# Second weight of an expert's last 32 of 288 tokens: 32-row fp32r products replaced by plain fp32 partial products at four column positions

## The chip, the cores and the metric

The kernel runs on one core of one Trainium2 chip. The metric is device microseconds from start to end of one execution. The engines are TensorE (PE; its weight loads are shown apart as PEld, its sequencer's own instructions as PEldq), VectorE (DVE), ScalarE (ACT), GpSimd (POOL) and SyncE (SP), which issues the large DMA transfers.

## The reference

Three stages: windowed attention with 32 global tokens per batch entry, a channel mix, and a routed layer of eight experts with one expert per token. The change concerns the last one:

```python
    logits = np.einsum('bsd,de->bse', x, w_gate)
    local_gate = 1.0 / (1.0 + np.exp(-np.einsum('bsd,de->bse', x, w_local).squeeze(-1)))
    ...
            if s == 0 or local_gate[b, s] < 0.5:
                e = fresh_e
            else:
                e = prev_e if prev_e >= 0 else fresh_e
            ...
            h = np.maximum(x[b, s] @ w1[e], 0.0)
            out[b, s] = p[e] * (h @ w2[e])
```

There are 4 x 544 = 2176 tokens of 512 numbers; `w1[e]` is 512x1024, `w2[e]` is 1024x512. How many tokens an expert has is known only on the chip, after routing.

## The kernel before

Attention, channel mix and routing fill the first 500 us or so, laid out by a scheduler at build time. Behind them the experts run one after the other, in an order written out by hand (class `Experts`).

**Three products for one.** A product of this stage keeps nearly fp32 accuracy by splitting both factors into a high part (rounded to fp32r) and a low part (the rest): `mm3` issues high x high, high x low and low x high into one PSUM tile, on lines 21, 23 and 24. Every such group of matmuls in the trace carries these three lines. `slot0h`/`slot0l` to `slot3h`/`slot3l` are the two parts of a weight matrix; an expert uses two slots (`w1` and `w2`) while the next expert's weights are converted into the other two.

**One expert.** `expert` first takes tokens by 32s: chains of `If` on the count `c` choose one arm. With 257 to 288 tokens that is `joined(288)`; other arms are `joined(320)`, `joined(352)`, `joined(256)`, `single`, `none` and `big`. Each of the five middle experts has the whole chain in its code. In this run expert 2 has 267 tokens and is the only one in `joined(288)`. The arm has these steps:

- `begin`: copies of indices, and the gather of the next expert's rows (L940, GpSimd).
- `wide`: the first weight, eight steps `f`; in each 12 matmuls of up to 288 columns into `ph`, then ScalarE writes the high part of relu (`hh`, L969) and VectorE the low part (`hl`, L970).
- `out_(0,e,2,slice(256,N))`: the second weight for the tokens from 256 on. `product` makes 24 matmuls whose stationary factor is 128 x 32 (32 tokens) and whose moving factor is the weight, 512 columns; `place` scales the rows by the gate's probability on VectorE (L1007, PSUM bank `po0` to `osb`) and scatters them from GpSimd (L1010).
- `second`: the same for tokens 128 to 255 into bank `po1`, 24 matmuls of 128 rows.

Then comes the jump out of the arm, L1066, taken by each engine's own sequencer. Behind the whole chain of `If`s, for all arms, stand the eviction of bank `po1` and the third product: tokens 0 to 127 into bank `po0`, with the next expert's last transposes (`third`, L955 and L956) inside. TensorE then goes on to the next expert's first weight.

**Weights meanwhile.** `W` is a list of weight parts of 128x1024 (`whole`). One takes a staged part (`st` or `sw`), converts the high half on ScalarE (L853), subtracts on VectorE or, for some, on GpSimd (L856), and issues the next load of 512 KB on SyncE (L843) into the staging tile just freed. Up to three parts are called inside `wide`, two inside `second` at `f` = 0 and 2, three in the third product.

The two lines that call the arm's second weight:

```python
            if N>256: s.out_(0,e,2,slice(256,N))
            second(W[:2])
```

## Time and profile before

| | |
|---|---|
| median of three runs (lowest, highest) | 728.1 us (727.04, 732.19) |
| the profiled execution | 728.47 us, span of its instructions 726.7 us |
| TensorE matmul busy | 671.5 us, 92% of the span |
| TensorE weight load busy | 573.6 us, 79% |
| VectorE, ScalarE, GpSimd busy | 459.0 (63%), 368.5 (51%), 316.5 (44%) us |
| mean granted TensorE clock | 0.966 |
| DMA | 76.36 MB, mean 105 GB/s |

The profile is one execution. Busy times are sums over overlapping records, so shares are averages over stages with different limits; in the expert stage TensorE has hardly any gap. A matmul's record is longer than the pace at which matmuls follow one another (0.39 us beside 0.23), since they overlap; costs are taken from the distance of starts. [...]

### The profile page before, as it was taken

What the parts mean: (1) busy time and instruction counts of PE and PEld (TensorE: products, weight loads), DVE (VectorE), ACT (ScalarE), POOL (GpSimd) and SP (SyncE); (2) the same over time, 40 slices, a digit from 0 to 9 for tenths busy, and PEclk for the clock granted to TensorE, in tenths of its full rate; (3) what the DMA queues carried; (4) which work ended last, traced back from release to release, by engine and by line L of the source; (5) the groups of instructions that cost most, each with busy time, mean ns of one, the idle gap of its engine ahead of it and who ended that gap; (6) DMA issues with size and microseconds to landing.
All of it is one profiled execution on the core that took longest, in us unless ns stands there. A gap on an engine that the chain in (4) does not pass through costs nothing. (4 is left out here: it accounts for less than half of the span.)

```text
span 726.7 us, 14139 instructions
## 1 busy us (share of the span) xinstructions
PE 671.5 (92%) x4890; PEld 573.6 (79%) x4890; DVE 459.0 (63%) x1370; ACT 368.5 (51%) x938; POOL 316.5 (44%) x446
## 2 busy tenths in 40 slices
PE   3876879899999999989998999999899999999996
PEld 2654668688897897878987898877688899989785
DVE  5587668867878588694478654786744426234461
ACT  4677666765465764556652423426553316125251
POOL 6486764833635437255224413204734414322441
PEclk9789879999999999999999999999999999999999
DMA  5766144153112332111051000318864705406530
GB/s 115 210 167 200 32 112 133 54 108 61 43 29 60 66 64 51 32 24 40 16 173 60 1 30 15 117 44 271 308 249 147 248 18 189 157 21 229 183 103 22
DMA packets 111743, 76.36 MB, mean 105 GB/s; under 512 B 88910, under 2 KB 93006, under 8 KB 111634
## 3 DMA queue, kind: packets, MB, share of 16 engines
q1 hardware_dynamic: 108178, 64.28, 30.9%
q0 software_dynamic: 3456, 10.75, 4.1%
q8 instruction: 53, 0.87, 0.5%
q14 instruction: 56, 0.46, 0.2%
HBM read 66.08 MB, written 9.44 MB: 104 GB/s over the span
## 5 line engine op out<-in xcount | busy, mean ns | idle before, releaser
L259 POOL TENSOR_SCALAR pl<-pl,mx 128x192 f32<-128x192 f32 (+1 forms) x128 | 68.4, 552 | 84.6 <-DVE mx L256 71.6
L21 PE MATMUL psk<-xs,slot0h 128*128 128x256 f32 x256 | 75.1, 296 | 0.0
L23 PE MATMUL psk<-xs,slot0h 128*128 128x256 f32 x256 | 74.2, 290 | 0.0
L24 PE MATMUL psk<-xs,slot0l 128*128 128x256 f32 x256 | 73.5, 288 | 0.0
L253 ACT ACTIVATE pl<-pl,mx 128x224 f32<-128x224 f32 (+1 forms) x128 | 58.6, 459 | 26.7 <-DVE mx L249 25.9
L511 POOL TENSOR_SCALAR xm<-xT,mut 128x256 f32<-128x256 f32 (+4 forms) x96 | 44.2, 479 | 52.4 <-DVE kl L531 16.0
L969 ACT ACTIVATE hh<-ph 128x256 fp32r<-128x256 f32 (+2 forms) x56 | 22.4, 400 | 73.5 <-PE ph L24 47.0
L518 POOL TENSOR_TENSOR xs<-xm,xs 128x512 fp32r<-128x512 f32 (+1 forms) x36 | 45.8, 1287 | 28.2 <-ACT xs L516 18.1
L21 PE MATMUL psv<-slot1h,kh 128*128 128x512 f32 x136 | 54.4, 403 | 0.2 <-DVE kr L527 0.2
L23 PE MATMUL psv<-slot1l,kh 128*128 128x512 f32 x136 | 54.1, 398 | 0.5 <-POOL slot1l L485 0.5
L24 PE MATMUL psv<-slot1h,kl 128*128 128x512 f32 x136 | 53.6, 395 | 0.0
L266 PE MATMUL ptp<-ident,pl 128*128 128x128 f32 x256 | 43.9, 296 | 7.7 <-POOL pl L259 3.7
L970 DVE SCALAR_TENSOR_TENSOR hl<-ph,hh 128x256 fp32r<-128x256 f32 (+2 forms) x56 | 24.7, 442 | 40.9 <-ACT hh L969 40.7
L21 PEld LDWEIGHTS psk<-xs,slot0h 128*128 128x128 f32 x256 | 49.8, 197 | 0.8 <-ACT xs L516 0.6
L23 PEld LDWEIGHTS psk<-xs,slot0h 128*128 128x128 f32 x256 | 49.5, 193 | 0.8 <-issue 0.5
L24 PEld LDWEIGHTS psk<-xs,slot0l 128*128 128x128 f32 x256 | 49.5, 193 | 0.0
L514 DVE SCALAR_TENSOR_TENSOR xm<-xT,mut,xm 128x256 f32<-128x256 f32 (+4 forms) x96 | 44.1, 497 | 4.8 <-POOL xm L511 4.7
L114 ACT ACTIVATE ph<-ptp 128x512 f32<-128x512 f32 x64 | 37.2, 587 | 15.3 <-PE ptp L266 15.1
L266 PEld LDWEIGHTS ptp<-ident,pl 128*128 128x128 f32 x256 | 31.1, 150 | 15.2 <-POOL pl L259 5.4
L940 POOL DMA_INDIRECT xs<-y,idx x23 | 26.0, 1130 | 34.3 <-DVE cint L766 18.4
L21 PE MATMUL ph<-xh,slot2h 128*128 128x256 f32 (+1 forms) x128 | 37.1, 290 | 2.3 <-issue 1.6
L24 PE MATMUL ph<-xh,slot2l 128*128 128x256 f32 (+1 forms) x128 | 36.5, 285 | 0.0
(613 smaller groups left out, 2167.8 us busy)
## 6 DMA issues: line engine op xcount, KB each, us to landing
st<-in_moe_w_dram SPq DMA_DIRECT2D x42, 512.0 KB, 4.8
sw<-in_moe_w_dram SPq DMA_DIRECT2D x22, 512.0 KB, 4.8
y<-r SPq DMA_DIRECT2D x17, 256.0 KB, 2.1
earlyh<-in_moe_w_k_dram SPq DMA_DIRECT2D x8, 512.0 KB, 4.0
raw<-in_moe_w_v_dram SPq DMA_DIRECT2D x8, 512.0 KB, 4.3
ve<-in_v_l_dram SPq DMA_DIRECT2D x32, 96.0 KB, 2.1
bq<-in_q_l_dram SPq DMA_DIRECT2D x16, 128.0 KB, 2.8
bk<-in_k_l_dram SPq DMA_DIRECT2D x16, 128.0 KB, 2.9
```

Of the source, the lines that this page charges most:

```text
L21: i=nc.tensor.matmul(out,wh,xh,start=first,stop=False)
L23: nc.tensor.matmul(out,wh,xl,start=False,stop=False)
L24: return nc.tensor.matmul(out,wl,xh,start=False,stop=last)
L114: s.made=nc.scalar.activation(out[0],x,AF.Copy).ins.name
L253: nc.scalar.activation(p[:,h,ks],p[:,h,ks],AF.Exp,bias=mx[:,h:h+1],scale=-1.0,accum_out=mx[:,4+h:5+h])
L259: nc.gpsimd.tensor_scalar(out=p[:,h,ks],in0=p[:,h,ks],scalar1=mx[:,6+h:7+h],scalar2=0.0,op0=ALU.mult,op1=ALU.add)
L266: nc.tensor.transpose(pt[:,c,h],p[:,h,c*96:c*96+P],s.ident)
L511: nc.gpsimd.tensor_scalar(out=x[:,u,o:o+k],in0=s.xT[b][:,c,q:q+k],scalar1=m[:,1,c:c+1],scalar2=0.0,op0=ALU.mult,op1=ALU.add)
L514: nc.vector.scalar_tensor_tensor(out=x[:,u,o:o+k],in0=s.xT[b][:,c,1+q:1+q+k],scalar=m[:,0,c:c+1],in1=x[:,u,o:o+k],op0=ALU.mult,op1=ALU.add)
L518: nc.gpsimd.tensor_sub(xl[:,cs,:n],x[:,:,:n],xh[:,cs,:n].bitcast(F32))
L940: s.nc.gpsimd.indirect_dma_start(out=s.xs[i][:,j,:],out_offset=None,in_=s.y,in_offset=IndirectOffsetOnAxis(ap=s.idx[:,ch:ch+1],axis=0))
L970: nc.vector.scalar_tensor_tensor(out=hl[:,f],in0=ph,scalar=0.0,in1=hh[:,f].bitcast(F32),op0=ALU.max,op1=ALU.subtract)
```

## The change

In `joined(288)` the separate product of the last 32 tokens goes away, with its eviction and scatter ahead of `second`. In its place `left` makes two closures, `parts` and `whole`. VectorE first adds `hh` and `hl` of those tokens to one plain fp32 tile `h` (128x8x32), and sums the identity over four blocks of 32 columns to a selection `sel` (128x32, a 1 where row and column agree modulo 32). `parts`, called inside the second product after `f` = 3, issues 16 plain fp32 products: chunks `f+0` to `f+3` of the hidden dimension go to four column positions of the array (rows 0, 32, 64, 96 of the PSUM tile `phl`), once with the weight's high and once with its low half, for `f` = 0 and 4. ScalarE copies the 128x512 partial sums to `osl`. `whole`, called after `f` = 6, multiplies `sel` with `osl` in one plain fp32 product (`phs`), which adds the four partial sums; VectorE scales by the probability and GpSimd scatters. The two weight parts stay at `f` = 0 and 2 of the second product.

```diff
--- before.py
+++ after.py
@@ -1013,6 +1013,28 @@
         return s.pcol[:,ch:ch+1],s.idx[:,ch:ch+1]
     def out_(s,b,e,c,js=slice(0,P),within={}):
         s.product(b,e,js,within); s.place(b,*s.cols(e,c),n=js.stop-js.start)
+    def left(s,e):
+
+        nc=s.nc; n=32; w2=s.views(e,1); hh,hl=[t[:,:,2*P:2*P+n].bitcast(F32) for t in s.h]; J=P//n
+        w=s.work.tile([P,512],F32,tag="osb",name="hw",bufs=2); h=w[:,:8*n].rearrange("p (f t) -> p f t",f=8); sel=w[:,8*n:9*n]
+        nc.vector.tensor_tensor(out=h,in0=hh,in1=hl,op=ALU.add)
+        nc.vector.tensor_reduce(out=sel,in_=s.ident.rearrange("p (j t) -> p t j",j=J),axis=X,op=ALU.add)
+        o=[]
+        def parts():
+            ps=s.ps.tile([P,512],F32,tag="ph",name="phl",bufs=4)
+            for f in range(0,8,J):
+                for q in range(2):
+                    for j in range(J):
+                        nc.tensor.matmul(ps[j*n:(j+1)*n],h[:,f+j],w2[q][:,f+j].bitcast(F32),start=f==0 and q==0,stop=f==8-J and q==1)
+            o.append(s.work.tile([P,512],F32,tag="osb",name="osl",bufs=2))
+            nc.scalar.activation(o[0],ps,AF.Copy)
+        def whole():
+            ps=s.ps.tile([P,512],F32,tag="ph",name="phs",bufs=4)[:n]
+            nc.tensor.matmul(ps,sel,o[0],start=True,stop=True)
+            pc,idx=s.cols(e,2); t=s.work.tile([P,512],F32,tag="osb",name="osb",bufs=2)[:n]
+            nc.vector.tensor_scalar(out=t,in0=ps,scalar1=pc[:n],scalar2=None,op0=ALU.mult)
+            s.scatter(t,idx[:n])
+        return parts,whole
     def one(s,i,e,b,W,X,o=None):
 
         W=list(W); n=3 if e==1 else 5; last=s.tall(i,e,[W.pop(0) for _ in range(min(n,len(W)))],lead=1 if e==1 else None)
@@ -1053,6 +1075,10 @@
         def joined(N):
             begin()
             s.wide(i,e,N,W[:3],X)
+            if N==WJ[0]:
+                parts,whole=s.left(e)
+                s.product(1,e,slice(P,2*P),{0:W[:1],2:W[:1],3:[parts],6:[whole]})
+                return
             if N>256: s.out_(0,e,2,slice(256,N))
             second(W[:2])
         def single():
```

How it moves instructions is seen in three places. TensorE, from the end of the first weight into the second weight, before (`po_6734` is bank `po0`, `po_6735` bank `po1`):

```order
L23 MATMUL po_6734<-slot0l,hh 32x512 [waits Pool_49]
L24 MATMUL po_6734<-slot0h,hl 32x512 [waits DVE_49]
L21 MATMUL po_6734<-slot0h,hh 32x512 [waits Activation_49]
L23 MATMUL po_6734<-slot0l,hh 32x512
L24 MATMUL po_6734<-slot0h,hl 32x512 [waits DVE_49]
L21 MATMUL po_6735<-slot0h,hh 128x512
L23 MATMUL po_6735<-slot0l,hh 128x512
```

The same engine in the changed kernel, from step `f` = 3 of the second product on (`hw` is the VectorE tile that holds `h` and `sel`):

```order
L21 MATMUL po_6735<-slot0h,hh 128x512 [waits Activation_49]
L23 MATMUL po_6735<-slot0l,hh 128x512
L24 MATMUL po_6735<-slot0h,hl 128x512
L1028 MATMUL phl<-slot0h,hw 32x512 [waits DVE_49]
L1028 MATMUL phl<-slot0h,hw 32x512 x3
L1028 MATMUL phl<-slot0l,hw 32x512 x4
L1028 MATMUL phl<-slot0h,hw 32x512 x4
L1028 MATMUL phl<-slot0l,hw 32x512 x2
L1028 MATMUL phl<-slot0l,hw 32x512 [waits Pool_49]
L1028 MATMUL phl<-slot0l,hw 32x512
L21 MATMUL po_6735<-slot0h,hh 128x512 [waits Activation_49]
L23 MATMUL po_6735<-slot0l,hh 128x512
```

The second product now follows the first weight directly, and the products of the 32 tokens stand in its middle, in place of 24 matmuls ahead of it.

TensorE at the end of the arm, before:

```order
L24 MATMUL po_6735<-slot0h,hl 128x512
L21 MATMUL po_6735<-slot0h,hh 128x512
L23 MATMUL po_6735<-slot0l,hh 128x512
L24 MATMUL po_6735<-slot0h,hl 128x512
L1066 UNCONDITIONAL_BRANCH
```

and in the changed kernel, where the jump has become line 1092:

```order
L21 MATMUL po_6735<-slot0h,hh 128x512 [waits Activation_49]
L23 MATMUL po_6735<-slot0l,hh 128x512
L24 MATMUL po_6735<-slot0h,hl 128x512
L1033 MATMUL phs<-osl,hw 32x512 [waits DVE_49,Activation_49]
L21 MATMUL po_6735<-slot0h,hh 128x512
L23 MATMUL po_6735<-slot0l,hh 128x512
L24 MATMUL po_6735<-slot0h,hl 128x512
L1092 UNCONDITIONAL_BRANCH
```

A product that waits for ScalarE's copy now stands four instructions ahead of the jump.

GpSimd in this arm, before (the two L940 rows are the gather of the next expert's rows):

```order
L940 DMA xs_5166<-y,idx 128x512 [waits DMASW1_49,PE_49]
L940 DMA xs_5166<-y,idx 128x512 [waits DMASW2_49,PE_49]
L1010 DMA out_dram<-osb,idx 2176x512 [waits DMASW3_49,DVE_49]
L856 TENSOR_TENSOR slot1l<-sw_6725,slot1h 128x1024 [waits DMAHW5_49,DMAHW0_49,Activation_49]
L1066 ISA [waits DMASW1_49]
L1066 UNCONDITIONAL_BRANCH
```

and in the changed kernel:

```order
L940 DMA xs_5166<-y,idx 128x512 [waits DMASW1_49,PE_49]
L940 DMA xs_5166<-y,idx 128x512 [waits DMASW2_49,PE_49]
L856 TENSOR_TENSOR slot1l<-sw_6725,slot1h 128x1024 [waits DMAHW5_49,DMAHW0_49,Activation_49]
L1010 DMA out_dram<-osb,idx 2176x512 [waits DMASW3_49,DVE_49]
L1092 ISA [waits DMASW1_49]
L1092 UNCONDITIONAL_BRANCH
```

The weight part and the scatter of the 32 tokens have changed places.

## Rows read from the trace of the kernel before

**Rows 1.** Stretch: us, busy us (records) per engine, PEclk, DMA share, GB/s

```profile
556.00:720.80 164.80, 162.89 (x994) 145.12 (x992) 69.60 (x102) 59.02 (x97) 54.27 (x42) 1.00 0.42 137
```

**Rows 2.** TensorE's waits, 500 to 727 us: total us, times, longest

```profile
PE pt L955 <- DMA xs<-y,idx: 1.9, 1, 1.9
PE ph L21 <- issue: 1.9, 2, 1.6
```

**Rows 3.** Stretch view of the last 32 tokens, bank po alone

```profile
538.99:544.51 5.52, 5.52 (x24) 2.68 (x24) 0.00 (x0) 1.00 0.62 230
```

**Rows 4.** TensorE's timeline behind two jumps: start, us, line, operation [idle <-releaser]

```profile
525.24 0.37 PE L21 MATMUL ph<-xh,slot2h 128*128 128x288 f32 x1 [0.71 <-ACT slot0h L853]
...
550.09 0.40 PE L21 MATMUL po<-slot0h,hh 128*128 128x512 f32 x1
```

**Rows 5.** TensorE's timeline: a plain fp32 product of 512 columns, alone

```profile
25.86 1.07 PE L336 MATMUL sga<-earlyl 128*64 128x512 f32 x2
26.77 0.25 PE L336 MATMUL sgb<-earlyl 128*64 128x32 f32 x2
```

**Rows 6.** TensorE's timeline: attention's value products in pairs

```profile
308.43 0.27 PE L279 MATMUL avg<-ve,ph 128*64 128x64 f32 x1
308.44 0.27 PE L284 MATMUL avg<-ve,ph 128*64 128x64 f32 x1
308.54 0.22 PE L279 MATMUL avg<-ve,ph 128*64 128x64 f32 x1
...
309.06 1.92 PE L284 MATMUL av<-ph,ve 128*64 128x128 f32 x32
310.91 0.33 PE L676 MATMUL psc<-ident,row 128*128 128x128 f32 x1
```

**Rows 7.** Timeline of TensorE, VectorE and ScalarE around the 32 tokens

```profile
540.12 0.45 DVE L970 SCALAR_TENSOR_TENSOR hl<-ph,hh 128x288 fp32r<-128x288 f32 x1
540.45 1.05 ACT L853 ACTIVATE slot3h<-st 128x1024 fp32r<-128x1024 f32 x1
...
544.28 0.40 PE L24 MATMUL po<-slot0h,hl 128*32 128x512 f32 x1
...
544.72 0.74 DVE L1007 TENSOR_SCALAR osb<-po,acc 32x512 f32<-32x512 f32 x1 [4.14 <-PE po L24]
...
552.11 0.60 ACT L956 ACTIVATE xh<-pt 128x512 fp32r<-128x512 f32 x1 [10.62 <-PE pt L955]
```

**Rows 8.** Line 1066, 545 to 547 us: ns min/median/max, first and last start

```profile
L1066 PEldq COMPARE_BRANCH  x1: 3244/3244/3244, 545.9 to 545.9; - x1
```

**Rows 9.** Timeline of the last expert's end: VectorE, then TensorE's weight load

```profile
717.38 0.69 DVE L982 TENSOR_TENSOR hl<-pht,hh 128x512 fp32r<-128x512 f32 x1 [2.45 <-ACT hh L981]
...
718.13 0.19 PEld L24 LDWEIGHTS po<-slot3h,hl 128*128 128x128 f32 x1
```

**Rows 10.** Stretches of four jumps of TensorE, from the branch record's start to end

```profile
520.56:525.07 4.51, 3.96 (x13) 2.90 (x11) 3.74 (x5) 3.44 (x4) 2.29 (x3) 0.66 0.89 304
545.93:549.18 3.25, 3.25 (x16) 2.62 (x15) 0.66 (x1) 0.00 (x0) 3.23 (x2) 1.00 0.05 12
679.90:685.61 5.71, 4.18 (x19) 3.05 (x17) 3.81 (x4) 3.44 (x4) 2.48 (x2) 1.00 0.82 256
718.19:721.88 3.69, 2.63 (x12) 1.81 (x10) 0.75 (x1) 0.00 (x0) 0.00 (x0) 1.00 0.03 7
```

**Rows 11.** GpSimd's timeline: the weight part behind the scatter

```profile
547.39 2.42 POOL L856 TENSOR_TENSOR slot1l<-sw,slot1h 128x1024 fp32r<-128x1024 f32 x1
```

**Rows 12.** DMA issues, 549.5 to 555.5 us: count, KB, us from issue to landing

```profile
sw<-in_moe_w_dram SPq DMA_DIRECT2D x1, 512.0 KB, 4.4
st<-in_moe_w_dram SPq DMA_DIRECT2D x1, 512.0 KB, 6.1
```

**Rows 13.** Stretches behind two gaps of TensorE, columns as in rows 1

```profile
685.70:690.00 4.30, 4.30 (x36) 4.30 (x37) 0.85 (x2) 0.77 (x2) 1.39 (x2) 1.00 0.87 300
520.95:523.60 2.65, 2.65 (x8) 2.13 (x7) 1.88 (x3) 2.27 (x3) 1.68 (x2) 0.50 0.89 313
```

## Prediction

> **What bounds the kernel now.** [...] Then its waits, from 500 us on: 1.9 us once for a gather before expert 2, 1.9 us in two pieces that no semaphore explains ("issue") [rows 2], and 0.71 us at the start of expert 2's first weight [rows 4]. So the experts are bound by TensorE's work, and by the places where TensorE has nothing issued to it. The changed branch runs once, for expert 2: the 24 matmuls of its last 32 tokens fill 538.99 to 544.51, 5.52 us without a hole, 0.23 us each [rows 3]. Behind them stand the 24 matmuls of the second product, then the jump out of the If arm, then the third product, whose first matmul starts at 550.09 with no idle time before it [rows 4]. That start is the number to move: everything after it is TensorE's chain to the end.

> **Removed.** 5.52 us of TensorE time [rows 3], one eviction on VectorE (it moves later, 32x512 again) and nothing else.

> **Added on TensorE, the partial sums.** 16 plain fp32 products of 512 moving columns. Such a product is two records in the trace. One alone, at one column position: two records from 25.86 until the next product's start at 26.77, 0.91 us, 0.455 each [rows 5]. What several column positions cost together is seen in the attention: its value products stand in pairs at two column positions (64 columns each), in plain fp32. The first record of the second product (L284) starts with the first record of the first (L279), before the latter's own second record [rows 6]; 32 records of 128 columns take 1.92 us, so 15 steps in 1.92 - 0.27 = 1.65 us, 0.11 us for a pair [rows 6]. Scaled to 512 columns a pair costs 0.44 us, no more than one record alone (0.455): two positions are wholly side by side. No row has four. Bounds: four side by side give 4 groups x 2 records x 0.44 = 3.52 us; two at a time 7.04; one after another 16 x 0.91 = 14.6. I take the first, since the nearest row shows no loss at two. The way in and out: the next full-width matmul starts at 310.91, 0.09 us later than the last step would ask for (309.06 + 16 x 0.11 = 310.82) [rows 6]; I take 0.1 for each side, so 3.7 us.

> [...]

> **Added, the sum over positions.** One fp32 product of 512 columns: 0.91 us [rows 5]. TensorE's own balance is 5.52 - 3.7 - 0.91 = 0.9 us gained.

> **Around it.** VectorE adds hi and lo (128x256) and sums the identity (128x32x4) behind the last hl, which ends at 540.57 [rows 7]. Neither operation has a row of its own; a 128x512 product on it takes 0.69 [rows 9], so I count 0.7 for both, bounds 0.3 and 1.4: 541.0 to 542.0. The parts are due after four of eight steps, 538.99 + 12 x 0.23 = 541.75, so this costs nothing, 0.2 at most. ScalarE is free from 541.50 [rows 7]. It copies the partial sums: an eviction starts about 0.2 us after the last matmul's stream ends (544.28 + 0.23 to 544.72) and a 128x512 one takes 0.60 [rows 7]. Three steps of the second product (2.1 us) stand between the parts and the sum, so the copy itself (0.8 us) is covered.

> **What is late next: the jump.** Here the gain meets something else. The branch at the end of the arm is taken by TensorE's sequencer at 545.9 and lasts 3244 ns [rows 8], that is until 549.18, while TensorE works off 18 matmuls issued ahead (550.09 - 545.93 = 4.16 us of them). Now the sum product waits for ScalarE's copy, with three matmuls behind it and then the jump. Does a waiting matmul hold the sequencer? At the kernel's end it does: VectorE's last hl ends at 717.38 + 0.69 = 718.07, the weight load that waits for it starts at 718.13, and the jump behind it starts at 718.19, though ten more matmuls had still to be issued and over two us of work to run [rows 9, 10]. So the jump cannot start before the copy is done:

> - parts begin 541.75, end 541.75 + 3.7 = 545.45 (without the way out 545.35)
> - copy done 545.35 + 0.2 + 0.60 = 546.15; with about 0.1 us from there to the jump, as in rows 9 and 10: 546.25
> - first matmul of the third product: 546.25 + J + 0.17, where J is the jump's length; the 0.17 is what lay between the end of the jump at 525.07 and the matmul that closed the 0.71 us wait at 525.24 [rows 4, 10]

> TensorE itself would be through at 545.45 + 2.1 + 0.91 + 0.7 = 549.15, so any J above 2.7 us leaves it idle. Against 550.09 the balance is J - 3.67: the change gains below 3.67 and loses above.

> **What J will be.** With the DMA engines at 0.05 or less of their time the jump took 3.25 and 3.69, with 0.82 and 0.89 it took 5.71 and 4.51 [rows 10]. Today's jump falls into a silent stretch, and the change fills it. On GpSimd the scatter of the 32 tokens stands ahead of a weight part (slot1l), which therefore runs at 547.39 [rows 11] though ScalarE had made its high half before it began the next one (slot3h) at 540.45 [rows 7]; only behind it SyncE sends two weight loads of 512 KB, landed 4.4 and 6.1 us after issue [rows 12]. The changed order puts the weight part first: 540.6 to 543.0, the loads from 543.0 and 543.5, on the way until 547.4 and 549.6. The jump from 546.25 on lies in the second half of that. I take J = 4.2, between the silent and the busy rows, nearer the silent ones because the load is tailing off. The balance is 4.2 - 3.67 = +0.5 us: the 0.9 gained in matmuls goes into some 1.5 us of idle time. [...]

> **Base.** The profiled execution took 728.47 us (span 726.7 and 1.8 around it), 0.4 above the median of the three runs, 728.1. The sum on its own base is 729.0; on the median 728.1 + 0.5 = 728.6.

> **Rivals.**
> 1. *The gain arrives* (not slower, a little faster). The jump is taken early or fast enough: J below 2.7, or the wait does not hold the sequencer there. Then 728.1 - 0.9 = 727.2. For it: TensorE has over 2 us of issued work at that point. Against it: rows 9, and no jump of this kind was under 3.2.
> 2. *Two positions at a time.* The parts take 7.04 + 0.2, the copy is done near 549.7, the DMA engines are calm again (J about 3.6): third product at 553.5, +3.4, 731.5. For it: nothing here shows more than two streams. [...]
> 3. *Packing with a loss*: halfway between my bounds of 3.52 and 7.04, so 5.28 us for the parts. Everything behind them is 1.76 later at the same J: 730.4. For it: four streams share what two did not have to share; against it only that two show no loss.
> 4. *A long jump and the clock*: J as in the busy rows, 4.5 to 5.7, gives +0.8 to +2.0, and an idle time near 3 us may halve the clock for some us as after the 1.9 us wait, 1.3 more (half of the 2.65 us in rows 13): 729 to 731.4.
> 5. *One after another*: 14.6 us of parts, third product at 560.6, +10.5, 738.6. It decides above 1% only if concurrency fails wholly. Against it rows 6.

> **Chances.** Four side by side with the gain eaten by the jump 0.58; rival 1 0.13; rival 2 0.11; rival 3 0.06; rival 4 0.09; rival 5 0.03. The likeliest is 728.6, its own range 727.7 (J 3.25) to 729.4 (J 4.5). The range that holds eight in ten runs from rival 1 to rivals 3 and 4, 727.0 to 731.0; it leaves out rivals 2 and 5 and the end of rival 4. 1% (7.3 us) is about what a measurement of this kernel can tell from no change. None of the cases gains that much and only rival 5 loses it: faster 0.01, same 0.95, slower 0.04.

> **What would show it.** In the profile after: sixteen fp32 products whose records start in fours about 0.44 us apart, over in about 3.7 us (twice that: rival 2). ScalarE's copy near 545.6. The branch record of TensorE's sequencer starting just after that copy ends, its length, and an idle time of TensorE ahead of the third product as long as J - 2.7. GpSimd's weight part near 540.6 and SyncE's two loads from 543. If the branch starts before the copy ends, my step from wait to jump is wrong; if J stays at 3.2 the loads do not slow the jump and 727.7 is right; if TensorE is idle at f = 3 of the second product, VectorE's two operations were too dear.

## The result and the profile after

The changed kernel took 733.04 us (median of 12 runs), the kernel before 728.01 in runs beside it. The ratio is 1.0051 with a 95% interval of 1.0028 to 1.0074: 2.0 to 5.4 us slower, 3.7 in the middle. The ratio is taken from fast runs, without one slow run of the changed kernel, and is smaller than that of the two medians, which are 5.0 us apart. The forecast was 0.5 us slower, 727.0 to 731.0. The sign was right. The size was not, and the median lies outside the range.

The profiled execution of the changed kernel has a span of 727.6 us, only 0.9 more than that of before. That comparison misleads. Expert 2's first weight began 2.6 us earlier in this execution (522.63, before 525.24 [rows 4]), and then took 1.5 us longer (15.27 us at granted clock 0.89, before 13.75 at 1.00). Both vary between two profiles of one kernel, too (c0_before: start 524.17, 15.26 us at 0.89; c1_after: 524.56, 13.75 us at 1.00). So stretches have to be compared, each from its own start. And one profile is one execution: this one took 729.28 us, 3.8 less than the median of its kernel.

First the arm itself. TensorE's and ScalarE's timelines of the changed kernel (start, us, engine, line, operation, and in brackets the idle time before it):

```profile
540.78 1.06 PE L1028 MATMUL phl<-slot0h,hw 128*32 128x512 f32 x8
...
544.35 0.50 PE L21 MATMUL po<-slot0h,hh 128*128 128x512 f32 x1
...
546.62 1.04 PE L1033 MATMUL phs<-osl,hw 128*32 128x512 f32 x2
547.59 0.50 PE L21 MATMUL po<-slot0h,hh 128*128 128x512 f32 x1
...
549.60 0.48 PE L21 MATMUL po<-slot0h,hh 128*128 128x512 f32 x1 [1.05 <-issue]
```

```profile
544.48 0.60 ACT L1030 ACTIVATE osl<-phl 128x512 f32<-128x512 f32 x1 [4.08 <-PE phl L1028]
```

The jump out of the arm, in the view of its line (ns min/median/max, then first and last start):

```profile
L1092 PEldq COMPARE_BRANCH  x1: 4287/4287/4287, 545.1 to 545.1; - x1
```

The 16 partial products take 3.57 us (540.78 to 544.35), the sum product 0.97 (546.62 to 547.59). ScalarE's copy ends at 545.08, the branch starts at 545.14 and lasts 4.29 us where it lasted 3.24 [rows 8], and TensorE stands idle for 1.05 us before the third product, where it had no idle time [rows 4].

Second, what lies behind. The stretch view of the changed kernel, columns as in [rows 1]: the arm from the end of the first weight to the third product, and from there to the last matmul:

```profile
537.90:549.60 11.70, 10.65 (x60) 5.28 (x59) 5.88 (x6) 2.90 (x4) 3.52 (x2) 1.00 0.60 198
549.60:721.73 172.13, 169.28 (x1020) 150.21 (x1020) 73.18 (x105) 62.40 (x101) 55.96 (x44) 1.00 0.40 132
```

and of the kernel before:

```profile
538.99:550.09 11.10, 11.10 (x50) 7.19 (x48) 3.46 (x4) 2.31 (x3) 4.05 (x2) 1.00 0.33 119
550.09:720.83 170.74, 168.83 (x1021) 149.98 (x1019) 73.35 (x105) 62.46 (x101) 55.65 (x43) 1.00 0.43 139
```

The arm is 0.60 us longer, as forecast. But 1.4 us more are lost behind it, where the same matmuls run as before. TensorE's waits of the changed kernel from 640 us on (total us, times, longest):

```profile
PE ph L21 <- issue: 2.4, 2, 1.5
PE po L21 <- issue: 0.4, 1, 0.4
```

The kernel before has one long wait of this kind there, 1.6 us [rows 2]. The changed one has two in expert 6's first weight (0.96 us where the jump into it ends, and 1.47), and one of 0.39 in expert 4's third product (the expectations below call it expert 5's; its matmul reads `slot0h`, ahead of the jump into expert 5). The 1.47 us in its timeline:

```profile
688.78 0.28 PE L21 MATMUL ph<-xh,slot2h 128*128 128x256 f32 x1 [1.47 <-issue]
```

No semaphore holds this matmul. Its weights were loaded before the gap (at 687.03, 0.19 us), so what is missing seems to be the instruction. It stands 19 weight loads behind the jump into expert 6's arm (679.77, 5.08 us long). That is where the experiments started.

### The profile page after: what moved, and what is told of

It is laid out like the page before. It is cut to its first block, busy times and chain, and to the rows that moved or that the text cites. A ratio compares the mean times of both kernels' runs of the same rounds, so it can differ in the third digit from the quotient of the medians.

```text
span 727.6 us, 14164 instructions
## 1 busy us (share of the span) xinstructions
PE 667.7 (92%) x4900; PEld 569.6 (78%) x4900; DVE 461.7 (63%) x1372; ACT 368.4 (51%) x939; POOL 316.3 (43%) x446
## 5 line engine op out<-in xcount | busy, mean ns | idle before, releaser
L21 PE MATMUL psk<-xs,slot0h 128*128 128x256 f32 x256 | 73.6, 290 | 1.2 <-ACT xs L516 1.2
L23 PE MATMUL psk<-xs,slot0h 128*128 128x256 f32 x256 | 73.5, 288 | 0.5 <-POOL xs L518 0.5
L21 PEld LDWEIGHTS psk<-xs,slot0h 128*128 128x128 f32 x256 | 48.5, 190 | 1.9 <-ACT xs L516 1.6
L23 PEld LDWEIGHTS psk<-xs,slot0h 128*128 128x128 f32 x256 | 48.7, 190 | 1.6 <-POOL xs L518 0.7
L266 PE MATMUL ptp<-ident,pl 128*128 128x128 f32 x256 | 42.0, 287 | 7.4 <-POOL pl L259 3.2
L940 POOL DMA_INDIRECT xs<-y,idx x23 | 26.0, 1132 | 36.6 <-DVE cint L766 18.4
```

The costliest lines, as they stand in the source:

```text
L21: i=nc.tensor.matmul(out,wh,xh,start=first,stop=False)
L23: nc.tensor.matmul(out,wh,xl,start=False,stop=False)
L266: nc.tensor.transpose(pt[:,c,h],p[:,h,c*96:c*96+P],s.ident)
L940: s.nc.gpsimd.indirect_dma_start(out=s.xs[i][:,j,:],out_offset=None,in_=s.y,in_offset=IndirectOffsetOnAxis(ap=s.idx[:,ch:ch+1],axis=0))
```

## The experiments

In the table (one profile for each row), *arm* is the time from the end of expert 2's first weight to the third product, *jump* the branch record at the arm's end, *rest* the time from there to the last matmul, *late* the place of the idle time behind the jump into expert 6 (in weight loads); the ratio of times has its 95% interval.

| kernel | arm | jump | rest | late | ratio |
|---|---|---|---|---|---|
| before, first profile | 11.10 | 3.24 | 170.74 | none | |
| c0_before | 11.11 | 3.25 | 170.89 | none | 1.0015 (0.9982 to 1.0048) |
| changed, first profile | 11.70 | 4.29 | 172.13 | 19 | 1.0051 (1.0028 to 1.0074) |
| c1_after | 11.78 | 4.37 | 173.98 | 19 | 1.0040 (1.0008 to 1.0072) |
| e2_unused | 11.10 | 0.95 | 172.70 | 19 | 1.0030 (1.0002 to 1.0058) |
| e3_nowait | 9.34 | 2.31 | 170.65 | 31 | 0.9986 (0.9961 to 1.0011) |
| e4_aligned | 10.50 | 2.08 | 170.11 | none | 1.0011 (0.9983 to 1.0039) |
| e11_aligned2 | 11.95 | 4.51 | 169.66 | none | 1.0018 (0.9997 to 1.0039) |
| e5_quiet | 11.20 | 3.78 | 169.65 | none | 1.0001 (0.9972 to 1.0029) |
| e9_quiet2 | 10.69 | 0.69 | 175.53 | 19 | 1.0036 (1.0009 to 1.0062) |
| e7_pad | 11.11 | 3.25 | 175.02 | 23 | 1.0053 (1.0018 to 1.0087) |
| e8_shift | 10.87 | 3.45 | 170.43 | none | 1.0034 (1.0007 to 1.0060) |
| e12_shift2 | 10.49 | 2.11 | 170.75 | none | 1.0027 (0.9997 to 1.0057) |
| e6_vsum | 9.35 | 2.72 | 169.99 | none | 0.9983 (0.9956 to 1.0011) |
| e10_vsum2 | 9.46 | 4.48 | 169.32 | none | 0.9969 (0.9935 to 1.0002) |

### Both kernels again, and the code without its execution

> The kernel before against itself, for the spread of a comparison and a second profile. All theories: ratio 1.000. In the arm of expert 2 the stretch from the end of the first weight to the first matmul of the third product is 11.1 us, as in the first profile (538.99 to 550.09). The stretches ahead of it (gather wait, jump into the arm, TensorE's clock behind them) may differ from profile to profile by 1 to 3 us if chance sets them.

> The changed kernel once more. Its first profile has 11.7 us from the end of the first weight to the third product, against 11.1 before, as forecast, while the measured difference is 3.7 us (2.0 to 5.4). Theory A (only the arm changed; the rest of the 3.7 is chance in the gaps behind other jumps and in the clock): the stretch is 11.6 to 12.2 us again, ratio 1.001 to 1.002. Theory B (the code of five arms is longer, so jumps take longer everywhere): ratio 1.005 again, with longer branch records in other experts. Theory C (the earlier weight loads disturb what comes later, a later gather or jump): ratio 1.005 again, with the loss behind the third product of expert 2.

e2_unused puts the new code into an arm that no expert takes:

```diff
-            if N==WJ[0]:
+            if N==WJ[1]:
```

> The same code, put into the arm for 289 to 320 tokens, which no expert takes in this run: the program is as long as the changed one, what runs is as before. Theory B: ratio 1.005, jumps longer. Theories A and C: ratio 1.000, and 11.1 us from the end of the first weight to the third product.

The kernel before against itself came out at 1.0015, so such a comparison is good to some 0.3%. The changed kernel showed the same two losses: arm 11.78, and an idle time at the very same matmul of expert 6. From c1_after's stretches (the first weight of expert 6 to the end, and the 5.4 us behind the gap) and its timeline:

```profile
685.13:724.07 38.94, 36.91 (x204) 32.14 (x204) 15.33 (x21) 13.71 (x22) 10.34 (x8) 0.96 0.29 98
689.56:695.00 5.44, 5.44 (x33) 5.43 (x33) 1.35 (x3) 1.85 (x4) 0.30 (x2) 0.69 0.14 54
```

```profile
689.56 0.28 PE L21 MATMUL ph<-xh,slot2h 128*128 128x256 f32 x1 [2.02 <-issue]
```

The gap of 2.02 us is followed by a granted clock of 0.69 on the mean of 5.44 us, so here it costs more than itself: 38.94 us, where before needs 35.16. In the changed kernel's first profile the gap of 1.47 left the clock at 1.00 and the stretch took 36.83. The same stretch before, then in the changed kernel's first profile:

```profile
685.67:720.83 35.16, 35.16 (x204) 30.52 (x204) 15.21 (x20) 13.71 (x22) 10.25 (x8) 1.00 0.30 100
684.90:721.73 36.83, 35.35 (x204) 30.61 (x204) 15.21 (x20) 13.71 (x22) 10.05 (x8) 1.00 0.29 99
```

e2_unused executes before's instructions and still has the loss behind the arm: rest 172.70, the same gap behind 19 weight loads (2.2 us). Its rest, then its waits from 640 us on:

```profile
552.85:725.55 172.70, 168.94 (x1021) 150.15 (x1019) 73.37 (x105) 62.45 (x101) 54.51 (x43) 1.00 0.42 138
```

```profile
PE ph L21 <- issue: 2.9, 2, 2.2
PE po L21 <- issue: 0.9, 1, 0.9
```

So theory B holds for the rest, in a changed form: jumps as such are not longer (into expert 6 5.08 us in the changed kernel's first profile, 5.71 before [rows 10]), something behind them comes late. Theory C falls, since the loads of this arm are before's. Behind this gap, longer than that of c1_after, the granted clock stayed at 1.00 on the mean of the rest. Its times (1.0030, 1.0002 to 1.0058) take in theory B's 1.005 and just leave out 1.000; the profile is plainer.

What comes late may be seen in the trace's DMA packets of kind "instruction". One queue (q8) moves 16 KB at a time: 53 packets, 0.87 MB in before's profile and in the changed kernel's first one. In these two, one such transfer starts 2.30 to 2.75 us ahead of the end of each of TensorE's jumps over 3 us, eight in each. In c1_after a transfer starts at 682.54 during the jump into expert 6 (which ends at 685.08) and the next at 687.20; the missing matmul runs at 689.56, 2.36 us after that start. The two windows hold one transfer each:

```profile
q8 instruction: 1, 0.02, 19.6%
```

```profile
q8 instruction: 1, 0.02, 37.7%
```

```profile
L1028 PEld LDWEIGHTS phl<-slot0h,hw x16: 106/110/110, 540.8 to 542.5; 128*32 128x32 f32 x16
L1028 PE MATMUL phl<-slot0h,hw x16: 592/592/617, 540.8 to 543.0; 128*32 128x512 f32 x16
...
L1033 PEld LDWEIGHTS phs<-osl,hw x2: 106/108/109, 546.6 to 546.6; 128*32 128x32 f32 x2
L1033 PE MATMUL phs<-osl,hw x2: 592/604/617, 546.6 to 547.1; 128*32 128x512 f32 x2
L1033 PEldq EVENT_SEMAPHORE  x1: 51/51/51, 542.5 to 542.5; - x1
```

With as many again on the weight's low half, that is 64 + 5 = 69 instructions in place of 24 x 2 = 48: 21 more for each of five experts, run or not. The target in expert 6 lies 5 x 21 = 105 instructions further on.

### The wait ahead of the jump

e3_nowait leaves out the sum product (VectorE scales a quarter of the sum):

```diff
-            ps=s.ps.tile([P,512],F32,tag="ph",name="phs",bufs=4)[:n]
-            nc.tensor.matmul(ps,sel,o[0],start=True,stop=True)
...
-            nc.vector.tensor_scalar(out=t,in0=ps,scalar1=pc[:n],scalar2=None,op0=ALU.mult)
+            s.nc.vector.tensor_scalar(out=t,in0=o[0][:n],scalar1=pc[:n],scalar2=None,op0=ALU.mult)
```

> The changed kernel without the product that adds the four partial sums: VectorE scales and scatters the first of them alone, so the 32 tokens get a quarter of their sum. TensorE has no wait ahead of the jump. If that wait holds the jump (theory A), the branch record now starts about 18 matmul records before the second product ends, 2 us earlier, and the stretch from the end of the first weight to the third product falls from 11.7 to 9.8 us or less; ratio 0.998. If the wait doesn't matter, only the 0.98 us of the product goes: 10.7 us. Theory B: still 1.004. Theory C: the loads are as early as in the changed kernel, so ratio 1.003.

The branch and ScalarE's copy in this kernel, whose first weight ended at 541.43:

```profile
L1090 PEldq COMPARE_BRANCH  x1: 2307/2307/2307, 546.2 to 546.2; - x1
```

```profile
548.01 0.60 ACT L1030 ACTIVATE osl<-phl 128x512 f32<-128x512 f32 x1 [4.08 <-PE phl L1028]
```

The branch starts 4.80 us behind the first weight's end, 1.8 us ahead of the copy. In both profiles of the changed kernel it starts 7.24 us behind, right after the copy. The wait does hold the jump. The arm falls to 9.34 us with no idle time: 2.36 less than 11.70, of which 0.97 is the product and 1.05 the idle time; the 0.3 left over may be the way into the product and out of it.

The run also gave a number that had not been asked for: its five instructions fewer per expert move expert 6's target back by 25, and the late matmul moves from 19 to 31 weight loads behind the jump, which is 24 instructions.

### The position of the code

e4_aligned takes ten matmuls out of the arm *single*, which no expert takes, so that per expert the code is 1 instruction longer than before, not 21. Expert 6's own *single* stands behind the target, so this target lies 5 x 21 - 4 x 20 = 25 instructions further on than before, not 105. What runs is the changed kernel word for word (`cut=5` in *single* alone):

```diff
+                if 4*b+d<cut: s.release(nc.tensor.matmul(ph,xh[:,d,:P],w1h[:,d,bs],start=d==0,stop=d==3))
+                else: s.release(mm3(nc,ph,xh[:,d,:P],xl[:,d,:P],w1h[:,d,bs],w1l[:,d,bs],d==0,d==3))
...
-            begin(); s.tall(i,e,W,X)
+            begin(); s.tall(i,e,W,X,cut=5)
```

> The changed kernel with ten matmuls fewer in the arm single, which no expert takes in this run: per expert TensorE's code is one instruction longer than before instead of 21, so what lies behind the arms stands nearly where it stood before against the 16 KB blocks in which TensorE's code is fetched; what runs is the changed kernel word for word. Theory B in its present form (the longer code moves the targets of later jumps against those blocks, and a second fetch comes too late): the idle time of 1.5 to 2.2 us twenty matmuls into expert 6 and the 0.4 to 0.9 us in expert 5's third product are gone, the stretch from the third product of expert 2 to the end is 170.7 to 171.0 us again, and 11.7 us in the arm of expert 2 stay: ratio 1.001. If code length is not the cause, 1.004 and both idle times stay.

> e4_aligned once more, next to e12_shift2 on one chip. Code position theory: no idle time behind the first 20 to 30 weight loads of expert 6; 169.7 to 170.5 us from expert 2's third product to the end, ratio 0.999 to 1.002. The jump out of expert 2's arm took 2.1 us in its first profile with its fetch under way before the branch; if that was chance of the DMA queues, it is 4.3 here and the stretch of the arm 11.7 us.

Twice the late matmul is gone and the rest is down to 170.11 and 169.66. The rest of e4_aligned, and all that is left of TensorE's waits from 640 us on, in e4_aligned, then in e11_aligned2:

```profile
551.07:721.18 170.11, 168.90 (x1021) 149.93 (x1019) 73.21 (x106) 62.48 (x101) 56.80 (x44) 1.00 0.41 134
```

```profile
PE ph L21 <- issue: 1.2, 2, 0.7
```

```profile
PE ph L21 <- issue: 0.7, 2, 0.6
```

The rest is even 0.7 and 1.2 us shorter than before's, because the jump into expert 6 left TensorE idle for 0.7 and 0.6 us, where before had 1.6 and 1.7. That wait is between 0.2 and 1.7 us in the profiles, so a rest is good to about 1 us. The arm, for which the expectation of e4_aligned had 11.7, came to 10.50 there and to 11.95 in e11_aligned2; that is the subject of the section on the jump.

The ratios, 1.0011 and 1.0018, are 0.8 and 1.3 us: near the forecast of 0.5, and 2.3 us less than the changed kernel's on the mean of two each. The single intervals overlap, so the times support the reading and the profiles carry it.

e7_pad is the counter-test: the kernel before, with twelve superfluous matmuls in *single* (24 instructions per expert, not run):

```diff
+                for _ in range(pad if b==0 and d==1 else 0): nc.tensor.matmul(ph,xh[:,d,:P],w1h[:,d,bs],start=False,stop=False)
...
-            begin(); s.tall(i,e,W,X)
+            begin(); s.tall(i,e,W,X,pad=12)
```

> The kernel before with twelve superfluous matmuls (24 instructions of TensorE) in each expert's arm single, which is not run: what runs is the kernel before. Code position theory: the target of the jump into expert 6 stands 4 x 24 = 96 instructions further on than before. In the changed kernel it stood 5 x 21 = 105 further and the fetch came too late behind 19 weight loads; in e3_nowait 5 x 16 = 80 further, and it was 31. So 96 gives idle time after about 24 weight loads, 1 to 2 us, and 171.5 to 173 us from expert 2's third product to the end instead of 170.8; ratio 1.002 to 1.003. If the change itself and not the position did it: no such gap, 1.000.

The kernel before became as slow as the changed one, 1.0053, and the gap came behind 23 weight loads (24 forecast). Its rest and the 5.2 us behind the gap, then its waits from 640 us on:

```profile
553.75:728.77 175.02, 170.90 (x1021) 151.53 (x1019) 73.46 (x105) 62.46 (x101) 55.65 (x43) 0.99 0.42 136
694.77:700.00 5.23, 5.23 (x31) 5.23 (x32) 2.11 (x4) 2.16 (x5) 0.30 (x2) 0.67 0.03 10
```

```profile
PE ph L24 <- issue: 2.0, 1, 2.0
PE ph L21 <- issue: 1.3, 1, 1.3
PE pt L955 <- issue: 0.9, 1, 0.9
```

The rest, 175.02 us, is 4.2 longer than before's mean, more than the 171.5 to 173 that were forecast; as in c1_after the granted clock was lower behind the gap, 0.67.

e8_shift lengthens the changed kernel's code further, by 12 instructions per expert (`pad=6`), so that by this reading the target falls into the next block:

> The changed kernel with six superfluous matmuls (12 instructions) in each arm single, not run. The target of the jump into expert 6 is 48 instructions further on than in the changed kernel, where about 40 lay between it and the end of its 16 KB block: it falls into the next block, with a nearly whole block behind it. Code position theory: the idle time twenty matmuls into expert 6 vanishes, and so does that in expert 5's third product (36 further on, 25 lay ahead of it), although the code is longer still; 170 to 171 us from expert 2's third product to the end, ratio 1.001 or less. Mere length theory: as bad as the changed kernel or worse, 1.004.

> e8_shift once more. Its profile showed no idle time behind the jump into expert 6, as the code position theory forecast, but its times stood at 1.0034 (1.0007 to 1.006), where that theory says 1.001 or less. If the first times were chance: 0.999 to 1.002 here, close to e11_aligned2. If a longer code costs something else besides: 1.003 again, and above e11_aligned2.

The profiles went as the position theory says: no late matmul in either, rest 170.43 and 170.75, with longer code than the changed kernel's. All that is left of the waits from 640 us on, in e8_shift, then in e12_shift2, is the one at the jump into expert 6:

```profile
PE ph L21 <- issue: 1.3, 1, 1.3
```

```profile
PE ph L21 <- issue: 1.7, 1, 1.7
```

The times did not: 1.0034 and 1.0027, where 1.001 was forecast. Both intervals reach down to 1.001 or below, and e11_aligned2 on the same chip stood at 1.0018, so it may be noise of this size. But the two agree with each other, and neither of the two profiles, of executions 1.8 and 1.3 us faster than the median, shows where 2 us would be. Also, e9_quiet2, with the late matmul and measured beside e8_shift, stood about as high (1.0036). Over the whole table, the five ratios of kernels with a gap behind 19 or 23 weight loads are between 1.0030 and 1.0053, the five of kernels with both the sum product and no late matmul (e4, e11, e5, e8, e12) between 1.0001 and 1.0034. So the late matmul follows the position of the code, and how much of the 3.7 us it makes up stays open.

### The loads and the jump

e9_quiet2 moves the two weight parts behind `f` = 7, so that their loads start behind the jump; e5_quiet does so on top of e4_aligned:

```diff
-                s.product(1,e,slice(P,2*P),{0:W[:1],2:W[:1],3:[parts],6:[whole]})
+                s.product(1,e,slice(P,2*P),{3:[parts],6:[whole],7:W[:2]})
```

> The changed kernel with its two weight parts called after f = 7 (their loads go out behind the jump's fetch) and the code's positions as in the changed kernel. If the weight packets delay the fetch for the jump out of expert 2's arm, its branch record falls from 4.3 to between 3.2 and 3.8 us and the stretch from the end of the first weight to the third product from 11.7 to between 10.6 and 11.2 us. If the position alone sets it (e4_aligned had 2.1 us with the loads under way): 4.3 and 11.7 again. Either way the later idle times of the changed kernel stay: ratio 1.003.

> As e4_aligned, and the two weight parts of the second product called after f = 7 instead of 0 and 2, so that their loads are issued after 548 us, behind the jump's fetch. If the weight packets delay the jump's fetch (0.9 us from the branch's start to the fetch in silent stretches, 1.9 to 2.0 in the changed kernel), the branch record falls from 4.3 to 3.2 to 3.4 us and the stretch from the end of the first weight to the third product from 11.7 to 10.7 us; ratio 0.999. If the fetch's delay has nothing to do with the loads: 4.3 and 11.7 again.

The arm came to 10.69 in e9_quiet2, as the loads' theory said, but by a jump of 0.69 us that neither theory had; to 11.20 with a jump of 3.78 in e5_quiet, where 10.7 and at most 3.4 were forecast. The late matmul stayed behind 19 weight loads in e9_quiet2 and the ratio at 1.0036, as forecast. The times do not tell anything about the loads. And the same code gave quite different jumps in two executions, all with the loads under way: 2.08 and 4.51 (e4_aligned, e11_aligned2), 3.45 and 2.11 (e8_shift, e12_shift2), 2.72 and 4.48 (e6_vsum, e10_vsum2). The branch in e4_aligned, then in e11_aligned2:

```profile
L1093 PEldq COMPARE_BRANCH  x1: 2083/2083/2083, 547.8 to 547.8; - x1
```

```profile
L1093 PEldq COMPARE_BRANCH  x1: 4511/4511/4511, 547.3 to 547.3; - x1
```

The instruction packets say what differs. In e11_aligned2 the 16 KB transfer starts 2.11 us behind the branch's start, in e4_aligned 0.31 us ahead of it; from there to the jump's end it is 2.40 us in both. At this jump the delay was 0.87 to 0.89 in three profiles of kernels with before's arm in silence, 1.42 in e5_quiet in silence, 1.03, 1.89, 1.98 and twice 2.1 with loads under way, and negative in the others. At this jump, delays near 2 us were seen only beside loads, so the packets probably slow the fetch when it comes after the branch. It isn't shown: one delay beside loads was 1.03, one in silence 1.42, and the run made to test it (e9_quiet2) had its fetch under way before the branch. Why the fetch is sometimes under way before the branch is taken, with the same code, is not settled.

### A version without the wait

e6_vsum drops the selection product. VectorE adds the four quarters straight from PSUM, scaled, with the code aligned as in e4_aligned (`cut=4`):

```diff
-            nc.tensor.matmul(ps,sel,o[0],start=True,stop=True)
...
+            nc.vector.tensor_scalar(out=t,in0=ps[:n],scalar1=pc[:n],scalar2=None,op0=ALU.mult)
+            for j in range(1,J): nc.vector.scalar_tensor_tensor(out=t,in0=ps[j*n:(j+1)*n],scalar=pc[:n],in1=t,op0=ALU.mult,op1=ALU.add)
```

> The changed kernel without the selection product: VectorE adds the four partial sums from PSUM by four operations of 32x512, scaled by the probability. Code aligned as in e4_aligned. Nothing on TensorE waits ahead of the jump. By the wait theory and e3_nowait: branch record starts 2 us or more earlier, no idle time before the third product, 9.3 to 9.8 us from the end of the first weight to it; ratio 0.998 with the aligned code. If VectorE's four operations (about 3 us) delay the low halves or conversions that TensorE needs next: idle time at the third product or at expert 3's first weight, ratio 1.000 or more.

> e6_vsum (sum of the parts on VectorE, aligned code) once more, for a second set of times: 9.3 us from the end of the first weight to the third product, 170.0 from there to the end; ratio 0.997 to 0.999 on the code position and wait theories together, 1.000 if its first result was chance.

VectorE's four operations in e6_vsum:

```profile
545.18 0.74 DVE L1032 TENSOR_SCALAR osb<-phl,acc 32x512 f32<-32x512 f32 x1 [1.22 <-PE phl L1028]
545.96 2.31 DVE L1033 SCALAR_TENSOR_TENSOR osb<-phl,acc,osb 32x512 f32<-32x512 f32 x3
```

They take 3.1 us in a stretch in which VectorE had time (busy for 7.49 of the arm's 9.35 us with them). The arm is 9.35 and 9.46 us with no idle time, whether the jump takes 2.72 or 4.48, since the branch starts 2.4 us earlier. The ratios are 0.9983 and 0.9969: 1.2 and 2.3 us faster than before in the middle. Each interval still holds 1.000, so this is a likely gain over before, not a shown one; against the changed kernel (1.0051 and 1.0040) the intervals do not touch in three of the four pairs.

## Why the prediction was wrong

- **Four positions side by side: right.** 3.57 us measured, 3.7 forecast. 16 products that would take 14.6 us one after another took 3.57, a factor of 4.1. For four column positions in plain fp32 the trace has the full factor. Rivals 2, 3 and 5 fell.
- **The sum product: right**, 0.97 for 0.91.
- **VectorE's preparation costs nothing: right.** `hw` was done at 540.25 (539.86 + 0.39), the parts began in their place at 540.78.
- **The wait holds the jump: right**, and shown by e3_nowait. The branch was forecast 7.26 us behind the first weight's end (538.99 to 546.25); it came at 7.24.
- **The jump of 4.2 us: right in the two profiles of the changed kernel** (4.29, 4.37), and the arm with them: 11.63 forecast (7.26 + 4.2 + 0.17), 11.70 and 11.78 measured. The figure was in part luck: the same instructions, with the code moved, gave 2.08 and 4.51, and the reason given for it, the loads, is likely and not shown. The arm's own share is between -0.6 and +0.85 us in the four profiles, 0.4 on their mean.
- **"Everything after it is TensorE's chain to the end": this step failed.** It took the 170.7 us behind the third product as fixed, because the instructions there were the same. They were, but not their positions: 21 more per expert in five copies of the arm moved the target of the jump into expert 6 by 105 instructions, and TensorE stood idle for 1.5 and 2.0 us 19 weight loads behind that jump, where by the reading above its block ran out; in one of the two profiles the granted clock was lower behind the gap (0.69). The rest is 1.3 and 3.2 us longer in these profiles (172.13 and 173.98 against 170.8); a smaller gap of 0.4 to 0.6 us in expert 4's third product is in it, and 0.6 to 1.1 us less of waiting where the jump into expert 6 ends. With the arm's 0.6 to 0.7 the sum is 1.9 and 3.8 us, beside 3.7 (2.0 to 5.4) measured. That the position makes the matmul late is shown by e2_unused, e3_nowait, e4_aligned and e7_pad; how much of the 3.7 us it is in a median execution is not, since e8_shift and e12_shift2 had no late matmul and were still 2.0 to 2.5 us slower than before. None of the rivals had the length of code that is not run, and the range left it out.
- **What would have shown it.** The profile of before has the "issue" waits of [rows 2] and jumps of 3.2 to 5.7 us [rows 10]; I read them as the price of a jump, and only asked what would make one jump longer. The question left out was how near to that edge the other jumps stand, and whether the change moves them.

## What to carry to other kernels

Where a kernel has long jumps and arms written out several times, a change is also a change of the place of all code behind it, in arms that never run too (ratio 1.0030 in e2_unused and 1.0053 in e7_pad, where before's instructions run). Before a difference of half a per cent is put down to the change, build a twin in which code that isn't run is lengthened or shortened so that the targets stand where they stood, and compare with that. A product that waits for another engine shortly ahead of a jump held the jump as well (branch 7.24 us behind the first weight's end, 4.80 without the product), so a sum that another engine has time for may be better made there (arm 9.35 and 9.46 us, beside 10.50 and 11.95 with the same alignment).

## What was unexpected of the hardware

- From the start of a 16 KB instruction transfer to the end of the jump during which it starts: 2.30 to 2.75 us in the eight jumps over 3 us of before's profile and the eight of the changed kernel's first one, with the DMA engines at 0.03 to 0.90 of their time. What varied was the start: 0.86 to 0.96 us behind the branch in the seven jumps with a DMA share of 0.03 to 0.05, 2.19 to 3.31 us in the four with 0.82 to 0.90.
- Behind eleven of these sixteen jumps the next transfer started 0.71 to 0.78 us after the jump's end, behind the others 1.10 to 2.31 us. Behind the jump into expert 6, where weights are loaded, it was 2.31 and 1.23 us in before's two profiles, and TensorE had no idle time behind the jump; in the changed kernel's two it was 1.46 and 2.12 us, and TensorE stood still for 1.47 and 2.02 us, until 2.48 and 2.36 us after the transfer's start.
- Plain fp32 products of 512 columns with 32 stationary columns, four at four column positions, took 0.45 us for four records (3.57 us for 32 in the changed kernel's first profile); one record alone took 0.455 [rows 5].
